# Spatial-reduction attention with a mixture of adapters: another order of the first batch's loads, scores and slots

## The chip, the cores and the metric

The kernel runs on one core of a Trainium2 chip. The metric is the device time of one execution in microseconds (us). Five engines run side by side, each through its own instructions in program order: TensorE (PE, with its weight loads listed as PEld), VectorE (DVE), ScalarE (ACT), GpSimd (POOL) and SyncE (SP, which here issues DMAs). They meet through semaphores. TensorE's products land in PSUM, and VectorE or ScalarE fetches them from there.

## The reference

Two layers, one behind the other. The first is attention whose keys and values are 4x4 means of a feature map times a matrix; keys and values are the same. The second is a mixture of eight low-rank adapters of which each token uses the two with the highest logits.

```python
B, C, Hh, Ww = (4, 128, 384, 32)          # q: (B, 12288, 128), kv: (B, 384, 32, 128)
kv_pool = kv.reshape(B, H // r, r, W // r, r, C).mean(axis=(2, 4))   # r = 4: 768 keys
kv_flat = kv_pool.reshape(B, -1, C) @ w_sr
s = (1 / sqrt(C)) * (q @ kv_flat^T);  a = softmax(s);  x = a @ kv_flat
...
logits = x @ w_gate                        # 8 adapters of rank 16
topk = the two largest;  w = softmax over these two
out = x + sum over the two of  w * (x @ A[e]) @ B[e]
```

## The kernel before, in words

**Tiling.** The 4 x 12288 queries are cut into 96 chunks of 512 (24 for each batch), and four chunks make a group of 2048 whose transposed queries lie in one qT tile. The 768 keys of a batch are three blocks of 256. A *score unit* `scores(k, r)` is chunk k against key block r: two matmuls of 128x512 into one of two score buffers `sg`, and one exponential of 128x1024 on ACT into `em[k]`. A chunk has three units. `attend(k, s)` multiplies a quarter of the chunk's `em` with the values `vx` (6 matmuls; 24 for the chunk) into the accumulator `acc`, of which there is only one. `normalize` (DVE: rinv, xn) frees it again. The columns behind the values give the softmax denominator and the logits' differences.

**A chunk's way after that.** `top` finds the largest logits (DVE, four MAX8). `route` and `gates` make the weights `gw`, for pairs of chunks on POOL with one tanh on ACT (chunks 0 and 1 on DVE). When a chunk *enters*, `transposes` turns its xn and the previous chunk's hg through PE into PSUM and one copy (DVE, line 346, or ACT, line 344) brings both back as `tts`. `down` (h_ps) multiplies with A and waits for this copy, `gate` (DVE, hg) multiplies with `gw`, a slot later `up` (d_ps) multiplies with B and `finish` adds and stores (DVE, osb, and a DMA on SP).

**Slots.** The main loop (line 430) runs one slot for each k. Its order on PE: first score unit; transposes; second unit; `up`; a quarter of the attend of the chunk before; third unit; `down`; three quarters of the attend. Everything is issued under `keep`, which holds an engine's instructions in the order of the program. Which chunks are attended and which enter in a slot is worked out ahead by the dictionaries `att` and `enter` (lines 413 to 426). Before the change the prologue does all three units of chunks 0 to 3, and the loop begins at slot 4. Slot 4 attends chunk 0, slot 5 chunk 1, slots 6, 7 and 8 two chunks each, and from slot 9 on slot k attends chunk k-1. Chunks enter six slots behind, and slots 73, 74 and 76 take two at a time.

**Prologue.** The loads go out on SP (lines 126 to 136): group 0 of q in one DMA of 1 MB, the 24 pieces (256 KB) of the first batch's kv, group 1 of q in four pieces. Groups 0 and 1 of q are transposed on PE in fp32 (`turn_q`, copies on ACT, line 117; group 1 partly inside slots 4 to 6); later groups are cast by a POOL DMA (`cast_q`) and transposed by an SP DMA (`load_qT`). For each key block DVE adds rows (line 184), PE transposes and sums the rest in PSUM (`keys`, kpT_ps), DVE scales (kpT), `keys2` makes kfT and `values` makes vx. The projection of w_sr and w_gate (lines 146 to 157) comes first of all on PE. Batches 1 to 3 are prepared by POOL and in later slots; the sums of batch 1 go to POOL from slot 8 on (line 506).

Of the kernel before, what the change touches and what calls it, by code (L numbers as in the profile page):

```python
# [10 lines left out]
FP32 = mybir.dt.float32  # L11
BF16 = mybir.dt.bfloat16
# [3 lines left out]
ALU = mybir.AluOpType  # L16
# [4 lines left out]
def kernel(  # L21
# [10 lines left out]
    nc = tc.nc  # L32
    P = 128
    B, N, C = q.tensor.shape
# [17 lines left out]
    kvpool = ctx.enter_context(tc.tile_pool(name="kvpool", bufs=3))  # L52
    per_b = ctx.enter_context(tc.tile_pool(name="per_b", bufs=2))
    qpool = ctx.enter_context(tc.tile_pool(name="qpool", bufs=4))
    ppool = ctx.enter_context(tc.tile_pool(name="ppool", bufs=7))
    xpool = ctx.enter_context(tc.tile_pool(name="xpool", bufs=1))
    rpool = ctx.enter_context(tc.tile_pool(name="rpool", bufs=4))
    gpool = ctx.enter_context(tc.tile_pool(name="gpool", bufs=6))
    run = ctx.enter_context(tc.tile_pool(name="run", bufs=3))
    opool = ctx.enter_context(tc.tile_pool(name="opool", bufs=6))  # L60
    qdram = ctx.enter_context(tc.tile_pool(name="qdram", bufs=1, space=bass.MemoryType.DRAM))
    ps_s = ctx.enter_context(tc.tile_pool(name="ps_s", bufs=2, space=bass.MemoryType.PSUM))
    ps_a = ctx.enter_context(tc.tile_pool(name="ps_a", bufs=1, space=bass.MemoryType.PSUM))
# [4 lines left out]
    def mm(*a, **k):  # L68
        return keep(nc.tensor.matmul(*a, **k))  # L69

    def mtile(shape, dtype=FP32, name="mb"):
        return ps_m.tile(shape, dtype, tag="mb", name=name)
# [10 lines left out]
    def load_qT(g):  # L83
        t = qpool.tile([P, GT], BF16, tag="qT", name="qT")
        keep(nc.sync.dma_start(t.rearrange("c (j p) -> c j p", p=P),
                               q_bf[g].rearrange("(p j) c -> p (j c)", p=P), transpose=True))
        qT[g] = t
# [11 lines left out]
            keep(nc.sync.dma_start(kvr[b, h][:, r, x], src[:, :, x * 4 * C:(x + 1) * 4 * C]))  # L99


    def load_q(g, lo, hi):
        if g not in q_f:
            q_f[g] = xpool.tile([P, GT // P, C], FP32, tag=f"qf{g}", name="qf")
        src = q[0, g * GT:(g + 1) * GT].rearrange("(p j) c -> p j c", p=P)
        keep(nc.sync.dma_start(q_f[g][:, lo:hi], src[:, lo:hi]))

    def turn_q(g, m, engine):
        if m == 0:
            qT[g] = qpool.tile([P, GT], BF16, tag="qT", name="qT")  # L110
        ps = mtile([P, S, P], name="qT_ps")
        for i in range(S):
            mm(ps[:, i], q_f[g][:, m * S + i], id_f, is_transpose=True,
               start=(i == 0), stop=(i == S - 1))
        o = qT[g][:, m * T:(m + 1) * T].rearrange("p (s t) -> p s t", s=S)
        if engine is nc.scalar:
            keep(nc.scalar.copy(o, ps))
        else:
            keep(nc.vector.tensor_copy(o, ps))

    q_f = {}
    w_sr_sb = const.tile([P, C], FP32)
    keep(nc.scalar.dma_start(w_sr_sb, w_sr))
    w_gate_sb = const.tile([P, E], FP32)
    keep(nc.scalar.dma_start(w_gate_sb, moe_w_gate))
    load_q(0, 0, GC * S)
    for h in range(3):
        for r in range(4):
            for x in range(2):
                load_kv(0, h, r, x)  # L130
    for m in range(GC):
        load_q(1, m * S, m * S + S)
    b_f = const.tile([P, C], FP32)
    keep(nc.sync.dma_start(b_f, moe_B.rearrange("e r c -> (e r) c")))
    a_f = const.tile([P, P], FP32)
# [7 lines left out]
    make_identity(nc, id_f)  # L143
    id_bf = const.tile([P, P], BF16)
    nc.vector.tensor_copy(id_bf, id_f)
    wext = const.tile([P, VC], FP32)
    nc.vector.tensor_copy(wext[:, 0:C], w_sr_sb)
    wT_ps = mtile([P, C], name="wT_ps")
    mm(wT_ps, w_sr_sb, id_f, is_transpose=True, start=True, stop=True)
    wT = const.tile([P, C], FP32)  # L150
    nc.vector.tensor_copy(wT, wT_ps)
    w2_ps = mtile([P, E], name="w2_ps")
    mm(w2_ps, wT, w_gate_sb, start=True, stop=True)
    w2 = const.tile([P, E], FP32)
    nc.vector.tensor_copy(w2, w2_ps)
    nc.vector.tensor_scalar(wext[:, C:VC], w2[:, 0:E - 1], w2[:, E - 1:E], None,
                            op0=ALU.subtract)


    ring = [xpool.tile([P, 2, S, C + E], FP32, tag=f"xr{i}", name="xn") for i in range(6)]  # L160
# [6 lines left out]
    def prepare(b, adder):  # L167
# [18 lines left out]
        for h in range(3):  # L186
            if adder is nc.vector:
                sums.append([lambda h=h, r=r, x=x: pair_step(h, r, x)
                             for r in (0, 2) for x in range(2)])
                continue  # L190
            sums.append([lambda h=h, step=step, lo=lo: pool_step(h, step, lo, lo + 512)
                         for step in range(5) for lo in range(0, 1024 if step < 3 else 512, 512)])

        st = {}

        def keys(h):
            if h == 0:
                st["kpT"] = prep.tile([P, J, P], FP32, tag="kpT", name="kpT")
                kfT[b] = per_b.tile([P, J, P], BF16, tag="kfT", name="kfT")
            kpT = st["kpT"]  # L200
            ps = mtile([P, 2, P], name="kpT_ps")
            if adder is nc.vector:
                parts = [(r, i, c) for r in (0, 2) for i in range(2) for c in range(4)]
            else:
                parts = [(0, i, 0) for i in range(2)]
            for n, (r, i, c) in enumerate(parts):
                mm(ps[:, i], kvr[b, h][:, r, i, c * C:(c + 1) * C], id_f, is_transpose=True,
                   start=(n == 0), stop=(n == len(parts) - 1))
            keep(nc.vector.tensor_scalar(kpT[:, 2 * h:2 * h + 2], ps, 1.0 / 16.0, None,
                                         op0=ALU.mult))  # L210

# [23 lines left out]
            keep(nc.vector.tensor_copy(kfT[b][:, 2 * h:2 * h + 2], ps))  # L235

        for h in range(3):
            for f in (keys, keys2, values) if adder is nc.vector else (keys, values, turn):
                rest.append(lambda h=h, f=f: f(h))
        return sums, rest  # L240

# [5 lines left out]
    def scores(k, r):  # L247
        b = k // NB
        if r == 0:
            em[k] = ppool.tile([P, J, T], FP16, tag="em", name="em")  # L250
        rhs = qT[k // GC][:, (k % GC) * T:(k % GC + 1) * T]
        ps = ps_s.tile([P, 2, T], FP32, tag="sg", name="sg")
        for i in range(2):
            mm(ps[:, i], kfT[b][:, 2 * r + i], rhs, start=True, stop=True)
        keep(nc.scalar.activation(em[k][:, 2 * r:2 * r + 2], ps, AF.Exp, bias=0.0, scale=scale))  # L255

    def attend(k, s):
        b = k // NB
        if s == 0:
            acc[k] = ps_a.tile([P, S, 256], FP32, tag="acc", name="acc")  # L260
        o = acc[k][:, s, 0:VE]
        for j in range(J):
            mm(o, em[k][:, j, s * P:(s + 1) * P], vx[b][:, j, 0:VE], start=(j == 0),
               stop=(j == J - 1))
# [112 lines left out]
        for d in (em, acc, xn, xT, hgT, hp, hg, dp):  # L377
            d.pop(k, None)

    LA = 4  # L380

    for m in range(GC):
        turn_q(0, m, nc.scalar)
    sums, rest = prepare(0, nc.vector)
    for h in range(3):
        for item in sums[h]:
            item()
        rest[3 * h]()
        if h > 0:
            scores(2, h - 1)  # L390
        rest[3 * h + 1]()
        if h > 0:
            scores(3, h - 1)
            rest[3 * h - 1]()
        scores(0, h)
        scores(1, h)
    rest[8]()
    scores(2, 2)
    scores(3, 2)
    rest = []  # L400

    late = const.tile([P, 1], FP32)
    keep(nc.gpsimd.tensor_copy(late, q_f[1][:, GC * S - 1, 0:1]))
    for g in range(2, 4):
        cast_q(g)
    a_bf = const.tile([P, P], BF16)
    keep(nc.vector.tensor_scalar(a_bf, a_f, 0.5, None, op0=ALU.mult))
    b_bf = const.tile([P, C], BF16)
    keep(nc.vector.tensor_copy(b_bf, b_f))
    turn_q(1, 0, nc.scalar)  # L410


    att = {LA: [0], LA + 1: [1], LA + 2: [2, 3], LA + 3: [4, 5], LA + 4: [6, 7]}
    for k in range(8, NCHUNK):
        att[k + 1] = [k]
    normed = {}
    for t, ks in att.items():
        for k in ks:
            normed[k] = t + 1 if k == ks[-1] else t
    ready = {k: normed[first[k] + size[k] - 1] + 1 for k in range(NCHUNK)}  # L420
    enter, t, left = {}, LA, list(range(NCHUNK - 3))
    while left:
        can = [k for k in left if ready[k] <= t]
        enter[t] = can[:2] if t in [NB * (B - 1) + 1 + i for i in (0,1,3)] else can[:1]
        left = [k for k in left if k not in enter[t]]
        t += 1

    sums, rest = [], []
    kh, ku, kd, kdone = [], [], [], []
    for k in range(LA, NCHUNK):  # L430
        b, i = divmod(k, NB)
        ka = att.get(k, [])
        kx = enter.get(k, [])
        if k % GC == 0:
            g = k // GC
            if 2 <= g + 1 < B * NG:
                load_qT(g + 1)
            if 4 <= g + 2 < B * NG and g + 2 not in q_bf:
                cast_q(g + 2)
# [12 lines left out]
                route(first[kn])  # L452

        kn = [n for n in att.get(k - 1, []) if normed[n] == k]
        if k == LA:
            for s in range(S):
                attend(0, s)
            ka = []
        scores(k, 0)
        while later:  # L460
            later.pop(0)()
        for x_ in kd:
# [3 lines left out]
        pairs = [(kx[j] if j < len(kx) else None, kh[j] if j < len(kh) else None)  # L466
                 for j in range(max(len(kx), len(kh)))]
        for x_, h_ in pairs[:1]:
            transposes(x_, h_, nc.vector)
        for x_ in kd:  # L470
            gate(x_)
        if k + 1 in range(GC + 1, 2 * GC):
            turn_q(1, (k + 1) % GC, nc.scalar)
        scores(k, 1)
        for u_ in ku:
            up(u_)
            finish(u_)
# [6 lines left out]
            attend(ka[0], 0)  # L484
        for n in kn:
            after_norm(n)
        scores(k, 2)
        for x_ in kx[:1]:
            down(x_)
            gate(x_)  # L490
# [15 lines left out]
                sums.pop(0)()  # L506

    K = NCHUNK - 1
    assert kh == [K - 3] and ku == [K - 4], (kh, ku)

    def bank(pool):
# [184 lines left out]
```

## Time and profile before

| | |
|---|---|
| median of 3 runs | 398.32 us (398.23 to 399.0) |
| the profiled execution | 400.91 us, its span 398.9 us |
| mean granted TensorE clock | 0.996 |
| score unit's exponential, ACT 128x1024 | 288 times, 1023 ns |
| transposes' copy, DVE 128x1024 (line 346) | 89 times, 692 ns |
| the same copy on ACT (line 344): 128x1024, 128x512 | 1012 ns, 585 ns |
| copy of q, ACT 128x512 (line 117) | 8 times, 608 ns |
| DVE add of two kv rows, 128x512 (line 184) | 12 times, 688 ns |
| the chain's end by engine | PE 84%, DVE 5%, ACT 3%, DMA 3% |

The span runs from the first to the last instruction; the time of the execution also has what lies around it. Times in the views are microseconds from the start of the span. A line of the timeline has the start, the length, the engine, the line of the kernel, the operation, what it writes and reads, how many instructions were merged, and in brackets how long the engine had been idle before and what ended that.

### The profile page before, as it was taken

The page shows a single profiled execution, that of the slowest core. Times are in us where ns is not written, and L with a number is a line of the kernel's source. Part 1 is how long each engine was busy: PE and PEld are TensorE (multiplying, and loading weights), DVE is VectorE, ACT ScalarE, POOL GpSimd, SP SyncE. Part 2 cuts the span into 40 slices and gives each one's busy share as a digit, 9 for nine tenths or more (in the row PEclk, how much of TensorE's full clock was granted, in tenths as well). Part 3 has the DMA queues.
Part 4 walks back from the last instruction along what each step waited for, and adds up shares of the span by engine and source line. Part 5 has one row for each costly group of instructions (what it writes and reads, how often), then busy time and mean ns, then how long its engine had stood idle before and what let it go on. Part 6 is the DMA issues. An engine that isn't in the chain of part 4 may idle for free.

```text
span 398.9 us, 11605 instructions
## 1 busy us (share of the span) xinstructions
PE 372.5 (93%) x4515; PEld 300.3 (75%) x4589; DVE 324.6 (81%) x945; ACT 297.0 (74%) x375; POOL 198.9 (50%) x457
## 2 busy tenths in 40 slices
PE   3898889999999999999999998999999899999993
PEld 2656777888878787887887886878786678788882
DVE  2553678899998889889898887988898788888885
ACT  2379467877787887787787876886878778888873
POOL 0010069887523486786523485787523344434443
PEclk9999999999999999999999999999999999999998
DMA  8988757993689999982679799993762847734113
GB/s 294 375 247 220 203 128 210 308 232 107 158 133 330 330 242 278 167 188 82 162 175 325 150 260 156 308 249 105 159 158 81 161 152 166 158 126 116 63 73 134
DMA packets 71463, 76.46 MB, mean 192 GB/s; under 512 B 49936, under 2 KB 50704, under 8 KB 70928
## 3 DMA queue, kind: packets, MB, share of 16 engines
q1 hardware_dynamic: 70272, 63.98, 57.6%
q0 software_dynamic: 704, 11.54, 15.0%
q8 instruction: 36, 0.59, 0.6%
q10 hardware_dynamic: 432, 0.20, 0.2%
q14 instruction: 19, 0.16, 0.1%
HBM read 50.53 MB, written 36.70 MB: 219 GB/s over the span
## 4 chain that ended last, share of the span: by engine, by line
PE 84%; DVE 5%; ACT 3%; DMA 3%; issue 2%; SPq 1%; POOL 0%; ACTq 0%; DVEq 0%; POOLq 0%
PE acc L69 33%; PE sg L69 24%; PE tt_ps L69 11%; PE h_ps L69 6%; PE d_ps L69 6%; ACT em L255 2%; DMA w_sr_sb<-in_w_sr_dram 1%; PE kpT_ps L69 1%; SPq L99 1%; DMA kvr<-in_kv_dram 1%; DVE rinv L268 1%; PE v_ps L69 1%; DVE xn L273 1%; DVE tts L346 1%; PE kfT_ps L69 1%
## 5 line engine op out<-in xcount | busy, mean ns | idle before, releaser
L255 ACT ACTIVATE em<-sg 128x1024 f16<-128x1024 f32 x288 | 280.4, 1023 | 78.7 <-PE sg L69 59.6
L69 PE MATMUL acc<-vx,em 128*128 128x136 f16 x2280 | 165.8, 223 | 2.8 <-issue 1.6
L69 PE MATMUL sg<-qT,kfT 128*128 128x512 bf16 x502 | 155.1, 379 | 2.9 <-ACT em L255 2.3
L69 PEld LDWEIGHTS <-em 128*128 128x128 f16 x2304 | 143.8, 98 | 4.9 <-DVE xn L273 2.2
L69 PEld LDWEIGHTS <-tts 128*128 128x128 bf16 x740 | 56.4, 98 | 46.1 <-issue 2.8
L273 DVE TENSOR_TENSOR xn<-acc,rinv 128x540 f32<-128x540 f32 x95 | 68.4, 720 | 3.3
L303 POOL TENSOR_TENSOR over<-xn,srt 128x64 f32<-128x64 f32 (+1 forms) x116 | 30.2, 281 | 79.7 <-DVE srt L291 79.7
L360 DVE TENSOR_TENSOR hg<-h_ps,gw 128x512 bf16<-128x512 f32 x93 | 64.3, 691 | 6.9 <-PE h_ps L69 0.2
L180 POOL TENSOR_TENSOR kvr<-kvr 128x512 f32<-128x512 f32 x54 | 67.3, 1271 | 0.0
L373 DVE TENSOR_TENSOR osb<-d_ps,xn 128x512 f32<-128x512 f32 x91 | 62.6, 691 | 0.6 <-PE d_ps L69 0.6
L346 DVE COPY tts<-tt_ps 128x1024 bf16<-128x1024 bf16 (+1 forms) x90 | 62.0, 689 | 1.2 <-ACT em L255 0.7
L324 POOL TENSOR_TENSOR gw<-th,over 128x64 f32<-128x64 f32 (+1 forms) x58 | 16.9, 291 | 73.1 <-ACT th L322 72.9
L69 PEld LDWEIGHTS <-kfT 128*128 128x128 bf16 x576 | 45.6, 98 | 6.3 <-issue 3.9
L268 DVE RECIPROCAL rinv<-acc 128x4 f32<-128x4 f32 x95 | 17.4, 183 | 35.8 <-PE acc L69 34.9
L69 PEld LDWEIGHTS <-xn 128*128 128x128 bf16 x384 | 29.1, 98 | 20.9 <-DVE xn L273 0.4
L69 PE MATMUL h_ps<-a_bf,tts 128*128 128x128 bf16 x372 | 36.0, 219 | 2.1 <-ACT tts L344 0.7
L69 PE MATMUL d_ps<-b_bf,tts 128*128 128x128 bf16 x364 | 35.2, 219 | 2.7 <-DVE tts L346 1.1
L69 PE MATMUL tt_ps<-id_bf,xn 128*128 128x128 bf16 x372 | 35.9, 219 | 1.2
L69 PE MATMUL tt_ps<-id_bf,hg 128*128 128x128 bf16 x368 | 35.6, 219 | 0.3 <-DVE hg L360 0.3
L291 DVE MAX8 srt<-xn 128x8 f32<-128x8 f32 x380 | 34.2, 153 | 0.2
L69 PEld LDWEIGHTS <-hg 128*128 128x128 bf16 x384 | 25.6, 98 | 1.3 <-DVE hg L360 0.5
L309 POOL TENSOR_SCALAR over<-over 128x64 f32<-128x64 f32 (+1 forms) x58 | 19.3, 333 | 5.2
(83 smaller groups left out, 198.1 us busy)
## 6 DMA issues: line engine op xcount, KB each, us to landing
out_dram<-osb SPq DMA_DIRECT2D x94, 256.0 KB, 3.6
kvr<-in_kv_dram SPq DMA_DIRECT2D x36, 512.0 KB, 6.8
qbf<-in_q_dram POOLq DMA_DIRECT2D x22, 512.0 KB, 7.5
kvr<-in_kv_dram SPq DMA_DIRECT2D x24, 256.0 KB, 5.3
qf<-in_q_dram SPq DMA_DIRECT2D x1, 1024.0 KB, 5.3
qf<-in_q_dram SPq DMA_DIRECT2D x4, 256.0 KB, 5.4
out_dram<-osb SPq DMA_DIRECT2D x3, 128.0 KB, 2.3
qT<-qbf SPq DMA_TRANSPOSE x22, 8.9
```

Source lines behind the costliest of these rows:

```text
L69: return keep(nc.tensor.matmul(*a, **k))
L180: keep(adder.tensor_tensor(u[:, lo:hi], u[:, lo:hi], v[:, lo:hi], op=ALU.add))
L255: keep(nc.scalar.activation(em[k][:, 2 * r:2 * r + 2], ps, AF.Exp, bias=0.0, scale=scale))
L268: keep(nc.vector.reciprocal(ri, acc[k][:, :, VC]))
L273: keep(nc.vector.tensor_tensor(x[:, :, 0:VC], acc[k][:, :, 0:VC], ri.unsqueeze(2).broadcast_to([P, S, VC]), op=ALU.mult))
L291: keep(nc.vector.max(srt[k0][:, m, s], xn[k][:, s, C:C + E]))
L303: keep(eng.tensor_tensor(d, lg, so[:, :, i].unsqueeze(2).broadcast_to([P, n, 8]), op=ALU.subtract))
L309: keep(eng.tensor_scalar(mask, mask, 0.0, None, op0=ALU.is_ge))
L324: keep(eng.tensor_tensor(w[:, 0:n], th, mask, op=ALU.mult))
L346: keep(nc.vector.tensor_copy(sb[:, lo:hi], ps[:, lo:hi]))
L360: keep(nc.vector.tensor_tensor(hg[k].rearrange("p s (e r) -> p (s e) r", e=E), hp[k].rearrange("p s (e r) -> p (s e) r", e=E), gw[k0][:, m ...
L373: keep(nc.vector.tensor_tensor(osb, dp[k], xn[k][:, :, 0:C], op=ALU.add))
```

## The change

The first batch is done in another order.

- **Loads:** the first key block goes ahead of everything (column half by column half); behind it come groups 0 and 1 of q in eight pieces of 256 KB, in tiles of the pool `opool`; then blocks two and three.
- **Spin:** fourteen matmuls of an identity with a tile of zeros stand first on PE. Their result isn't read.
- **Projection:** it becomes a function `project`, called among the first scores.
- **q:** `turn_q` transposes into halves of the one `acc` tile, and DVE makes all eight copies.
- **Key rows:** of a block's second column half only rows 0 and 1 are added on DVE; rows 2 and 3 are both transposed and summed on PE (20 transposes instead of 16, three sums instead of four).
- **Prologue's scores:** block one for chunks 0 to 7, block two for chunks 0 to 4, block three for chunk 0: 14 units instead of 12.
- **Slots:** the loop begins at slot 1 and each slot k attends chunk k-1. Slots 1 to 11 hold two score units, taken from a list; from slot 12 on three, as before. In slots below 12 the copy of the transposes is made by ACT.
- **Entering:** the planner's dictionaries follow: chunks enter four slots behind, and only slot 74 takes two.
- `load_qT(2)` is issued ahead of the loop, `late` (which holds back the first casts) waits for the last kv piece, and `ppool` and `opool` have 8 buffers.

```diff
-    ppool = ctx.enter_context(tc.tile_pool(name="ppool", bufs=7))
+    ppool = ctx.enter_context(tc.tile_pool(name="ppool", bufs=8))
...
-    opool = ctx.enter_context(tc.tile_pool(name="opool", bufs=6))
+    opool = ctx.enter_context(tc.tile_pool(name="opool", bufs=8))
...
+    def load_q(g, m):
+        q_f[g, m] = opool.tile([P, S, C], FP32, tag="osb", name="qf")
         src = q[0, g * GT:(g + 1) * GT].rearrange("(p j) c -> p j c", p=P)
-        keep(nc.sync.dma_start(q_f[g][:, lo:hi], src[:, lo:hi]))
+        keep(nc.sync.dma_start(q_f[g, m], src[:, m * S:(m + 1) * S]))
...
+    def turn_q(g, m):
         if m == 0:
             qT[g] = qpool.tile([P, GT], BF16, tag="qT", name="qT")
-        ps = mtile([P, S, P], name="qT_ps")
+        if m % 2 == 0:
+            turned[g] = ps_a.tile([P, 2, S, P], FP32, tag="acc", name="qT_ps")
+        ps = turned[g][:, m % 2]
...
+        keep(nc.vector.tensor_copy(
+            qT[g][:, m * T:(m + 1) * T].rearrange("p (s t) -> p s t", s=S), ps))
...
+    load_first(0)
+    for g in range(2):
+        for m in range(GC):
+            load_q(g, m)
+    load_first(1)
+    load_first(2)
...
+    zero = const.tile([P, T], BF16)
+    nc.vector.memset(zero, 0.0)
+    for _ in range(14):
+        mm(mtile([P, T], name="spin_ps"), id_bf, zero, start=True, stop=True)
+
     wext = const.tile([P, VC], FP32)
...
+    def project():
+        keep(nc.vector.tensor_copy(wext[:, 0:C], w_sr_sb))
+        wT_ps = mtile([P, C], name="wT_ps")
+        mm(wT_ps, w_sr_sb, id_f, is_transpose=True, start=True, stop=True)
...
             if adder is nc.vector:
                 sums.append([lambda h=h, r=r, x=x: pair_step(h, r, x)
-                             for r in (0, 2) for x in range(2)])
+                             for r, x in ((0, 0), (2, 0), (0, 1))])
...
+        def turn_rows(h, x):
+            if x == 0:
+                st["ps"] = mtile([P, 2, P], name="kpT_ps")
+            rows = (0, 2) if x == 0 else (0, 2, 3)
+            for r in rows:
+                for c in range(4):
+                    mm(st["ps"][:, x], kvr[b, h][:, r, x, c * C:(c + 1) * C], id_f,
+                       is_transpose=True, start=(x == 0 and r == 0 and c == 0),
+                       stop=(x == 1 and r == 3 and c == 3))
...
+            if adder is nc.vector:
+                rest.append([lambda h=h: turn_rows(h, 0), lambda h=h: turn_rows(h, 1),
+                             lambda h=h: keys(h), lambda h=h: keys2(h), lambda h=h: values(h)])
+                continue
...
+    first_sums(0, 0, 1, 2)
+    prep_of(0, 0, 1, 2)
+    turn_q(0, 0)
+    prep_of(0, 3)
+    turn_q(0, 1)
+    scores(0, 0)
+    turn_q(0, 2)
+    scores(1, 0)
+    turn_q(0, 3)
+    project()
+    scores(2, 0)
+    turn_q(1, 0)
+    prep_of(0, 4)
+    scores(3, 0)
+    turn_q(1, 1)
+    scores(4, 0)
+    turn_q(1, 2)
+    turn_q(1, 3)
+    first_sums(1, 0, 1)
+    scores(5, 0)
+    prep_of(1, 0)
+    first_sums(1, 2)
+    scores(6, 0)
+    scores(7, 0)
+    prep_of(1, 1, 2, 3)
+    scores(0, 1)
+    first_sums(2, 0, 1)
+    prep_of(1, 4)
+    scores(1, 1)
+    scores(2, 1)
+    prep_of(2, 0)
+    first_sums(2, 2)
+    scores(3, 1)
+    prep_of(2, 1, 2)
+    scores(4, 1)
+    prep_of(2, 3)
+    prep_of(2, 4)
+    scores(0, 2)
 
     late = const.tile([P, 1], FP32)
-    keep(nc.gpsimd.tensor_copy(late, q_f[1][:, GC * S - 1, 0:1]))
+    keep(nc.gpsimd.tensor_copy(late, kvr[0, 2][:, 3, 1, 0:1]))
...
+    load_qT(2)
+
+    units = [(5, 1), (1, 2), (2, 2), (6, 1), (3, 2), (7, 1), (4, 2), (5, 2), (6, 2), (7, 2)]
+    units += [(k, r) for k in range(8, NCHUNK) for r in range(R)]
+
+    def unit():
+        scores(*units.pop(0))
+
+    att = {k: [k - 1] for k in range(1, NCHUNK + 1)}
...
-        enter[t] = can[:2] if t in [NB * (B - 1) + 1 + i for i in (0,1,3)] else can[:1]
+        enter[t] = can[:2] if t == NB * (B - 1) + 2 else can[:1]
...
-    for k in range(LA, NCHUNK):
+    for k in range(1, NCHUNK):
...
-        scores(k, 0)
+        unit()
...
-            transposes(x_, h_, nc.vector)
+            transposes(x_, h_, nc.scalar if k < 12 else nc.vector)
...
-        scores(k, 1)
+        unit()
...
-        scores(k, 2)
+        if k >= 12:
+            unit()
```

## The prediction

> **What bounds the kernel now.** I read the page's busy shares and slices first, then the table of stretches, then the chain of waits in order of time, then the timeline of two places: the first 30 us, and the slots around 315 us.
>
> ```profile
> span 398.9 us, 11605 instructions
> PE 372.5 (93%) x4515; PEld 300.3 (75%) x4589; DVE 324.6 (81%) x945; ACT 297.0 (74%) x375; POOL 198.9 (50%) x457
> ...
> ACT  2379467877787887787787876886878778888873
> ...
> PE 84%; DVE 5%; ACT 3%; DMA 3%; issue 2%; SPq 1%; POOL 0%; ACTq 0%; DVEq 0%; POOLq 0%
> ```
>
> TensorE is the bound of nearly the whole span. The stretches (length, then busy time of PE, PEld, DVE, ACT, POOL, granted clock, DMA share, GB/s) show where it isn't:
>
> ```profile
> 0.00:5.00 5.00, 0.00 (x0) 0.00 (x0) 0.06 (x1) 1.49 (x2) 0.91 (x12) 1.00 0.63 209
> 35.00:40.00 5.00, 4.79 (x45) 3.54 (x46) 1.45 (x5) 5.00 (x8) 0.00 (x0) 1.00 1.04 297
> 45.00:50.00 5.00, 4.35 (x58) 3.51 (x60) 3.69 (x15) 1.92 (x2) 0.55 (x2) 1.00 0.36 106
> 60.00:70.00 10.00, 9.89 (x125) 7.87 (x125) 8.85 (x26) 7.32 (x11) 9.35 (x18) 1.00 0.76 210
> ```
>
> From slot 9 on PE is 99% busy. So only three places can pay: the prologue (to 29.95, where slot 4 begins), slots 4 to 8, and slots 73 to 79, as the chain shows (start, length, what):
>
> ```profile
> 62.68 1.06 PE acc L69 x18
> 66.35 1.06 PE acc L69 x18
> 69.96 1.06 PE acc L69 x18
> ...
> 296.43 1.07 PE acc L69 x18
> 300.04 0.71 PE acc L69 x12
> ...
> 331.20 1.06 PE acc L69 x18
> ```
>
> This piece comes 2.71 us after its slot's first score matmul (59.98 in slot 10), so slot 12 starts at 67.25. A plain slot is 3.61. From slot 72's piece (296.43) to slot 80's (331.20) eight slots take 34.77 instead of 28.88: three slots with two chunks entering cost 5.9 together.
>
> **The change, step by step.** After slot 11 both kernels have done 36 score units and attended chunks 0 to 10, and from slot 12 the slots hold the same work. So the forecast is: slot 12's new start against 67.25, less what slots 73 to 79 give back.
>
> *Loads.* The same 8.4 MB, in another order. Old: the eighth kv piece, with 1.05 MB of q ahead, lands at 12.3 (the sum at 12.35 waited for it), the fifteenth at 17.2: 0.71 us a piece. With no q ahead the first block is in 1.05 MB, or four pieces, earlier: 9.4. Query pieces then land from 10.1 to 15.1, blocks two and three are complete at 20.8 and 26.4 as before. Three more SP issues of about 0.6 hide behind the landings that pace that queue (uncovered: 1.8). The `late` copy now waits for the last kv piece, about 26.1 either way. SP waits for the first cast at load_qT(2); behind it stand only batch 1's loads and the first stores, slots away. Deeper ppool and opool issue nothing.
>
> *Fourteen spin matmuls.* PE has nothing to do before about 6.4. Half a score unit is 0.21, so 3.0 at full rate, 6.0 at half; from 2.2 they end at 5.2 to 8.2. Cost 0 to 0.6, taken 0. The weight loads of the first transposes took 229 ns until 12.9 and 140 ns after, though the granted clock reads 1.00 throughout.
> The Trainium skill (TensorE: Matmul & The Clock Gate, Part 4: PE-mode transpose) says that transposes don't count as activity and don't bring the full clock; here it rose after 5.7 us of nearly nothing but transposes, so the row disagrees. By the page, the 28 transposes between spin and first scores would fall back to slow ones, up to 28 x 0.09 = 2.5 us; by the row, none.
>
> *First scores.* Rows now need a sum of rows 0 and 1 only in the second half, and 12 transposes of 0.14 there: PE finishes them at about 10.4, kpT starts at 10.6. From there the old trace gives the rest:
>
> ```profile
> 12.35 0.69 DVE L184 TENSOR_TENSOR kvr<-kvr 128x512 f32<-128x512 f32 x1 [0.84 <-DMA kvr<-in_kv_dram]
> ...
> 14.08 0.42 DVE L209 TENSOR_SCALAR kpT<-kpT_ps 128x256 f32<-128x256 f32 x1 [1.04 <-PE kpT_ps L69]
> ...
> 15.36 0.42 DVE L216 CAST kfT<-kfT_ps 128x256 bf16<-128x256 f32 x1 [0.85 <-PE kfT_ps L69]
> ...
> 16.49 1.94 ACT L255 ACTIVATE em<-sg 128x1024 f16<-128x1024 f32 x2 [4.53 <-PE sg L69]
> ```
>
> kpT to first exponential is 2.41, so 13.0 instead of 16.49: 3.5 won.
>
> *The way to block two's scores.* From here I place the instructions one after another on their engines, in program order, with the rows' durations. Eight 128x512 copies of q leave ACT (0.61 each) for DVE. DVE has no such row; its 128x256 casts take 0.425 and the 128x512 adds out of PSUM 0.69, so 0.69. From 11.8 to block two's first sum DVE must do seven of these (4.83), the kfT and vx copies (0.87) and the projection (0.23 + 0.29 + 0.17 + 0.23): 6.6. It also waits. All turns go through the single acc buffer, two to a tile, so the third, fifth and seventh wait for both copies before them and then need 0.57 + 0.15 on PE: 2.0 of DVE waiting. The projection, formerly at 6.3 beside the first loads, puts a PE-DVE-PE-DVE trip among the scores: 0.7. Smaller gaps behind v_ps and score units: 0.9. So 22.1; without any waits 18.5, the lower bound. Then two sums (1.24), 4 transposes (0.56), units (6,0) and (7,0) (0.86), 12 transposes (1.68), 0.15: kpT at 26.6, exponential (0,1) at 29.0. The data lay there at 20.8; the old kernel had block two's scores at 21.39.
>
> *Block three.* From that unit's matmul (28.3): v_ps and (1,1) to 29.8, unit (2,1) waits for a score buffer until 30.1, then 8 transposes, (3,1), 12 transposes: 33.7. kpT, kfT and its copy: (0,2) at 35.5, slot 1 at 36.0. The same placing of the old prologue gives slot 4 at 30.98 against 29.95 in the trace, so I take 1.0 off: **slot 1 at 35.0** (31.4 if no wait on DVE were real).
>
> *Slots 1 to 11.* Dropping a unit leaves PE 3.61 - 0.43 = 3.18. But the copy behind the transposes goes to ACT, in line behind the slot's first exponential, and `down` needs it before three quarters of the attend. A row of that kind exists:
>
> ```profile
> 314.89 1.01 ACT L344 COPY tts<-tt_ps 128x1024 bf16<-128x1024 bf16 x1 [0.36 <-PE tt_ps L69]
> ...
> 315.96 0.40 PE L69 MATMUL h_ps<-a_bf,tts 128*128 128x128 bf16 x4 [0.53 <-ACT tts L344]
> ```
>
> So: first score to exponential 0.67, exponential 0.95 (back to back), copy 1.01, hand-over 0.05, `down` 0.22, 18 attends 1.07: 3.97, 0.8 above PE's work. Slots 4, 7, 9, 11: 3.97 each. Slots 8 and 10 have a tanh (0.15) between: 4.12. Slot 3 copies a half (0.585): 3.55. Slot 6 is 3.55 plus 0.4, because the tanh of pair 2 waits on ACT for POOL after slot 5. Slot 5, no `down`: 2.73. Slot 1 waits 0.88 for a score buffer: 3.17. Slot 2 has two units and an attend that waits 0.3 for its accumulator: 2.58. Sum 40.1 (old, slots 4 to 11: 37.3). **Slot 12 at 75.1, 7.8 late.** Bounds: with the copy hidden 33.2 (slots 4 and 7 to 11 at 3.18, slot 6 at 2.95, slot 3 at 2.73); with no overlap of back-to-back exponentials (0.07 on each of 22) 41.6.
>
> *Later.* Chunks enter two slots earlier, so two of three doubled entries go. One costs what rows of slots 73, 74, 78 and 79 show over 3.61: 0.22 + about 1.0 + 0.22 + 0.51 = 1.9. Given back: 5.9 - 1.9 = 4.0. Entering two slots earlier also takes a cover off: in even slots POOL's gw is ready 2.72 into the slot, where DVE starts hg at 2.81. Old slack two slots, new slack 0.09. I cost it at nothing; DVE's own reserve is 0.28 a slot (3.61 less 0.18 + 0.72 + 4 x 0.09 + 3 x 0.69).
>
> **Sum:** +7.8 - 4.0 = +3.8 on the span of 398.9, whose execution took 400.91. That lies 2.6 above the median of 398.32; the difference carries over: **402.1**.
>
> **Rivals.**
> *The first batch keeps pace with its loads* (faster). If DVE's waits shrink to what the loads demand, block three is done 26.4 + 0.7 + 2.4 = 29.5 and slot 1 starts near 30: -5, 397.1. For: ACT gives up eight copies; 3.5 us are won at the front. Against: everything is in program order on two engines that take turns. It decides if block two's sums start by 18.
> *The ACT copy is hidden* (faster). If it ends 1.9 into the slot, slots 1 to 11 take the 33.2 of above: -6.9, 395.2. For: ACT is only 74% busy. Against: the 0.53 wait at 315.96.
> *hg waits for gw* (slower still). If the gates come 0.4 late in even slots, 0.12 beyond the reserve over 30 slots is +3.6, and behind POOL's four 1.24 us sums up to 2 in a few: 406 to 408. It decides from 0.3 late. For: slack 0.09; against: in the last batch chunks already enter without slack and slots stay 3.61.
> *The spin does not bring the clock*: transposes stay 0.09 slower until 12.9, +0.6 to +1.5, 403.
>
> **How the numbers follow.** Forecast 402.1, own range 399.8 to 404.5, chance 0.57; first rival 0.13, second 0.08, third 0.14, spin 0.08. One 1.6 us gap marked "issue" at 246.15, if it goes, is inside the own range. Half measures of the first two rivals end between 398 and 400. I leave a tenth on each side: 397 to 406.5. A measurement tells 0.2%, 0.8 us, from no change: below 397.5 0.19, within 0.05, above 0.76.
>
> **What would show it.** First exponential near 13 and slot 1 near 35, block two's first sum near 21 to 22 although its rows lie there by 18; h_ps released by ACT tts about 0.9 late in slots 4 and 6 to 11; slot 12 near 75; one bulge near slot 75. Wrong if slot 1 starts before 32, if these slots take 3.3, or if hg lists POOL gw as a releaser.

## The result, and the profile after

| | before | after |
|---|---|---|
| median | 398.35 us (398.23 to 399.0, 4 runs) | 411.14 us (410.69 to 411.75, 4 runs) |
| ratio to before, 95% interval | | 1.0319 (1.0301 to 1.0337) |
| profiled execution, its span | 400.91 us, 398.9 us | 411.75 us, 409.9 us |
| mean granted TensorE clock | 0.996 | 0.997 |

The changed kernel is 12.8 us slower. The forecast was 3.8 slower, with 406.5 as the upper end of the range: the side was right, the size was not. The experiments ran on three chips (e1 to e4, e5 to e8, e9 to e11), where some executions of every kernel were disturbed and took several us more; beside each ratio the text therefore names the lowest group of times, which for the kernel before was 398.4 to 399.5 on all three.

The page's first part and the row of ACT in the slices, after:

```profile
span 409.9 us, 11667 instructions
PE 376.7 (92%) x4541; PEld 300.5 (73%) x4615; DVE 325.3 (79%) x945; ACT 298.2 (73%) x373; POOL 199.6 (49%) x457
...
ACT  1055776777777788778777887786877888888874
...
PE 81%; DMA 6%; DVE 5%; ACT 4%; issue 2%; SPq 1%; POOL 0%; ACTq 0%; DVEq 0%; POOLq 0%
PE acc L69 30%; PE sg L69 22%; PE tt_ps L69 10%; PE h_ps L69 6%; PE d_ps L69 5%; DMA qT<-qbf 4%; PE kpT_ps L69 2%; ACT em L281 2%; PE spin_ps L69 1%; ACT tts L370 1%; PE v_ps L69 1%; DMA kvr<-in_kv_dram 1%; DVE rinv L294 1%; PE qT_ps L69 1%; PE kfT_ps L69 1%
```

Busy times hardly moved: DVE has 0.7 us more, ACT 1.2, PE 4.2 (the spin is 5.7, so the rest has less). The other 6.8 us of the span's 11.0 are idle time of PE (33.2 instead of 26.4). The loss lies at the start: ACT stands at 5 tenths or less in the first four slices of 10.2 us, where before it stood at 2, 3, 7 and 9. The chain's shares would mislead here: PE's part fell from 84% to 81% and DMA's rose from 3% to 6%, but 4 of these 6 (qT<-qbf) are one transposed load far behind the prologue, for which PE waits 2.05 us at 278 (last section). The timeline of the first 20 us shows it one instruction at a time (start, length, engine, line, what; in brackets the idle time before and what ended it):

```profile
4.84 0.69 DVE L197 TENSOR_TENSOR kvr<-kvr 128x512 f32<-128x512 f32 x1 [3.68 <-DMA kvr<-in_kv_dram]
...
7.28 0.69 DVE L197 TENSOR_TENSOR kvr<-kvr 128x512 f32<-128x512 f32 x1 [1.75 <-DMA kvr<-in_kv_dram]
8.68 0.69 DVE L197 TENSOR_TENSOR kvr<-kvr 128x512 f32<-128x512 f32 x1 [0.71 <-DMA kvr<-in_kv_dram]
9.29 0.22 DVE L151 CAST id_bf<-id_f 128x128 bf16<-128x128 f32 x1
...
9.57 5.66 PE L69 MATMUL spin_ps<-zero,id_bf 128*128 128x512 bf16 x14 [9.57 <-DVE id_bf L151]
...
15.16 2.38 PE L69 MATMUL kpT_ps<-id_f,kvr 128*128 128x128 f32 x20
...
19.91 1.02 ACT L281 ACTIVATE em<-sg 128x1024 f16<-128x1024 f32 x1 [16.80 <-PE sg L69]
```

The reader is to see the order on DVE. The identity that the spin multiplies with is cast (line 151) *behind* the three sums of block one, and the sums wait for loads. So the spin, which stands first on PE, starts at 9.57 instead of about 2, and keeps the finished rows of block one waiting until 15.2. The first exponential comes at 19.91; the old kernel had it at 16.49.

From there the delay is carried. In the chain of waits slot 12's attend piece begins at 85.00, 2.70 after the slot's first score matmul, which puts slot 12 at 82.30 (67.25 before, 75.1 forecast):

```profile
69.51 1.06 PE acc L69 x18
73.43 1.06 PE acc L69 x18
77.48 1.07 PE acc L69 x18
81.39 1.08 PE acc L69 x18
...
85.00 1.07 PE acc L69 x18
...
311.83 1.06 PE acc L69 x18
...
342.45 1.07 PE acc L69 x18
```

The first five pieces are those of slots 8 to 12: 3.92, 4.05 and 3.91 apart where the forecast had 4.0 to 4.1 and PE's own work is 3.18; the fourth gap, 3.61, is that of a plain slot. Slot 80's piece (342.45) stands 11.25 behind the old one (331.20), slot 12's stood 15.04 behind: 3.8 came back in between. From slot 72's piece (311.83) to slot 80's the kernel takes 30.62, before 34.77, so the slots there give back 4.15; 0.4 of it is lost again on the way, where after has the wait of 2.05 at 278 and before a stall of 1.6 at 246.

### The profile page after: what moved, and what is told of

The parts are those of the page before. It is cut to its first block, busy times and chain, and to the rows that moved or that the text cites. A ratio compares the mean times of both kernels' runs of the same rounds, so it can differ in the third digit from the quotient of the medians.

```text
span 409.9 us, 11667 instructions
## 1 busy us (share of the span) xinstructions
PE 376.7 (92%) x4541; PEld 300.5 (73%) x4615; DVE 325.3 (79%) x945; ACT 298.2 (73%) x373; POOL 199.6 (49%) x457
## 4 chain that ended last, share of the span: by engine, by line
PE 81%; DMA 6%; DVE 5%; ACT 4%; issue 2%; SPq 1%; POOL 0%; ACTq 0%; DVEq 0%; POOLq 0%
PE acc L69 30%; PE sg L69 22%; PE tt_ps L69 10%; PE h_ps L69 6%; PE d_ps L69 5%; DMA qT<-qbf 4%; PE kpT_ps L69 2%; ACT em L281 2%; PE spin_ps L69 1%; ACT tts L370 1%; PE v_ps L69 1%; DMA kvr<-in_kv_dram 1%; DVE rinv L294 1%; PE qT_ps L69 1%; PE kfT_ps L69 1%
## 5 line engine op out<-in xcount | busy, mean ns | idle before, releaser
L372 DVE COPY tts<-tt_ps 128x1024 bf16<-128x1024 bf16 x84 | 58.1, 692 | 2.4 <-PE tt_ps L69 2.4
```

Source lines behind the costliest of these rows:

```text
L372: keep(nc.vector.tensor_copy(sb[:, lo:hi], ps[:, lo:hi]))
```

## Experiments

The first theory (A in the expectations) says that the spin's place, not its length, cost the unforeseen time: `keep` pins an instruction behind those before it on its engine, the identity's cast isn't kept and nothing pins the sums behind it, so it slid behind instructions that wait for loads. Its rival is that the spin itself is the loss, wherever it stands. A second group of runs asks for the price of two forecast costs (ACT's copy, the turns of q), a third for what the lag, the spin and the loads' order are worth.

### e1: identity and zeros kept in place

```diff
-    nc.vector.tensor_copy(id_bf, id_f)
+    keep(nc.vector.tensor_copy(id_bf, id_f))
-    nc.vector.memset(zero, 0.0)
+    keep(nc.vector.memset(zero, 0.0))
```

> The one difference to the changed kernel: the cast of the identity and the zeros are held in place on DVE, ahead of the first key sums, so the spin can start near 2 us and not at 9.57. Theory A (the late spin holds up the whole prologue): first score matmul near 12.5 instead of 19.27, everything behind it as much earlier, 404.3 us (404 to 405). Theory B (the prologue is bound by loads or by the DVE/PE chain anyway, the spin is hidden): first score earlier, but slot 1 within 2 us of before, 409 us or more.

Measured: 404.88 us median (lowest group 404.6 to 405.0, a fourth execution 412.75), ratio to before 1.0141 (1.0100 to 1.0182). Its timeline:

```profile
1.51 0.23 DVE L151 CAST id_bf<-id_f 128x128 bf16<-128x128 f32 x1 [0.65 <-POOL id_f masks.py:199]
...
2.06 6.02 PE L69 MATMUL spin_ps<-zero,id_bf 128*128 128x512 bf16 x14 [2.06 <-DVE zero L153]
...
9.46 0.69 DVE L197 TENSOR_TENSOR kvr<-kvr 128x512 f32<-128x512 f32 x1 [0.76 <-DMA kvr<-in_kv_dram]
...
14.43 1.02 ACT L281 ACTIVATE em<-sg 128x1024 f16<-128x1024 f32 x1 [11.31 <-PE sg L69]
```

Two kept instructions bring 6.3 us between the medians. The first exponential moves by 5.48 (19.91 to 14.43), slot 12 by 5.46 (to 76.84); the rest lies behind slot 12, where after's profile has its wait of 2.05 and e1's has none. The zeros were early in after as well (0.89), so it is the cast that counts. Theory A holds, and its rival falls: the spin ends at 8.08, inside the 5.2 to 8.2 that the prediction gave it, and hides behind the loads, since the last awaited sum starts only at 9.46. The first score came 1.3 later than theory A had expected (13.80, not 12.5).

### e2: the spin taken out

```diff
-    for _ in range(14):
-        mm(mtile([P, T], name="spin_ps"), id_bf, zero, start=True, stop=True)
```

> The changed kernel without its fourteen spin matmuls. Theory A1 (the spin, in time, saves slow transposes): the first 20 transposes run at 0.23 us, first score near 14.5, 406 us, slower than with an early spin by 1.5 to 2. Theory A2 (the spin buys nothing even when early): the same as with the early spin, 404 to 404.5. Theory B (spin hidden): no change, 411.

Measured: four executions of 405.47, 405.64, 411.48 and 569.47 us, ratio 1.0207 (1.0097 to 1.0318). The two low ones are 5.6 under after's median, and 0.8 over e1's lowest group. So the late spin was the loss. That an early one is better than none isn't shown here, as 0.8 is less than the interval can tell; e7 asks again.

### e3 and e4: the copy of the transposes on DVE

```diff
-            transposes(x_, h_, nc.scalar if k < 12 else nc.vector)
+            transposes(x_, h_, nc.vector)
```

e3 has this on top of e1, e4 on the changed kernel alone.

> Early identity as in the run before it, and the copies of the transposes in slots below 12 on DVE instead of ACT. My slot sum says slots 4 and 6 to 11 fall from 3.9-4.1 to 3.0-3.9, DVE-bound near 3.3 in the last four: slots 1 to 11 in 35.1 instead of 40.0, so 4.9 below the run with the early identity, 399.4 us. Rival: DVE, now at 3.3 of work a slot, and the single accumulator take it back: less than 2 us gained.

> The changed kernel with only the copies of slots below 12 moved from ACT to DVE, the spin as late as it was. If the two costs add, 4.9 below the changed kernel: 406.2 us. If the late prologue had hidden part of the slots' cost, less.

Measured: e3 400.35 us median (lowest group 399.0 to 399.4), ratio 0.9999 (0.9963 to 1.0036); e4 405.70 (lowest 404.95), ratio 1.0185 (1.0107 to 1.0262). Slot 12 starts 5.76 earlier than in e1 and 5.38 earlier than in the changed kernel, and the lowest times are some 5.5 lower, so this cost and the spin's add up. Slots 6 to 11 shrink from 3.91 to 4.06 each to 2.95 to 3.18, which is PE's own 3.18. In the changed kernel the wait reads so:

```profile
64.00 1.01 ACT L370 COPY tts<-tt_ps 128x1024 bf16<-128x1024 bf16 x1
...
65.06 0.40 PE L69 MATMUL h_ps<-a_bf,tts 128*128 128x128 bf16 x4 [0.79 <-ACT tts L370]
```

A part is given back behind slot 12: slot 13 takes 4.13 in e3 (74.69 to 78.82) where a plain slot takes 3.61. With the shorter slots two chunks' gates come while POOL still has sums of batch 1 in its queue, and there the third rival appears:

```profile
71.15 1.26 POOL L191 TENSOR_TENSOR kvr<-kvr 128x512 f32<-128x512 f32 x1
72.38 0.56 POOL L329 TENSOR_TENSOR over<-xn,srt 128x64 f32<-128x64 f32 x2
...
74.69 0.59 PE L69 MATMUL sg<-qT,kfT 128*128 128x512 bf16 x2
74.75 0.32 POOL L351 TENSOR_TENSOR gw<-gw,over 128x64 f32<-128x64 f32 x1
...
75.11 0.69 DVE L386 TENSOR_TENSOR hg<-h_ps,gw 128x512 bf16<-128x512 f32 x1 [1.32 <-POOL gw L351]
...
75.85 0.34 PE L69 MATMUL tt_ps<-id_bf,hg 128*128 128x128 bf16 x3 [0.34 <-DVE hg L386]
```

The gates of the pair start at 72.38, behind a sum of 1.26, and DVE's hg waits 1.32 for them; PE, which turns this hg in slot 13, has to wait in its turn, and slot 14 starts 0.5 late.

### e5 and e6: separate PSUM buffers for the turns of q

e5 is e3 with the odd turns in a buffer of their own; e6 is e5 with their copies on ACT.

```diff
-        ps = turned[g][:, m % 2]
+        ps = mtile([P, S, P], name="qT_ps") if m % 2 else turned[g][:, 0]
...
-        keep(nc.vector.tensor_copy(
-            qT[g][:, m * T:(m + 1) * T].rearrange("p (s t) -> p s t", s=S), ps))
+        o = qT[g][:, m * T:(m + 1) * T].rearrange("p (s t) -> p s t", s=S)
+        keep(nc.scalar.copy(o, ps) if m % 2 else nc.vector.tensor_copy(o, ps))
```

(The change of the copy, the two removed and the last two added lines, is in e6 alone.)

> Early identity and DVE copies in the slots (the 399 us version), and now every second turn of q has a PSUM buffer of its own instead of the other half of the acc tile. In that version each turn waited for the DVE copy of the turn before it, also within one tile, 1.44 us a turn. Theory (the shared tile serialises PE and DVE): turns 0.7 to 1.1 us apart, block two's first sum some 2 to 3 us before 24.15, 397 us. Rival (DVE's own 6.6 us of work sets it): less than 0.8 gained.

> As the run with the separate buffers, and every second copy of q is made by ACT. By the durations, block two's first exponential comes about 1.2 us earlier again and slot 1 with it: 395.5 to 396.5 us, faster than the kernel before. Rival: ACT's copies delay the first exponentials as much as DVE gains: no change to the run with separate buffers.

Measured: e5 396.58 us median (lowest group 396.2 to 396.6), ratio 0.9936 (0.9892 to 0.9980). e6 397.47 median of executions that scatter more, its lowest group 394.7 to 395.3, ratio 0.9918 (0.9875 to 0.9962). Block two's first sum is where they differ; the timelines of e3, e5 and e6, one line of each:

```profile
24.15 1.88 DVE L197 TENSOR_TENSOR kvr<-kvr 128x512 f32<-128x512 f32 x3
```

```profile
21.17 1.88 DVE L197 TENSOR_TENSOR kvr<-kvr 128x512 f32<-128x512 f32 x3
```

```profile
19.84 1.89 DVE L197 TENSOR_TENSOR kvr<-kvr 128x512 f32<-128x512 f32 x3
```

In e1 and e3 nearly every turn waits for the copy of the turn before, although the two write different halves of one tile. In e1's timeline PE and DVE take turns at 1.44 us a turn (0.66 and 0.69 with two hand-overs):

```profile
14.75 0.66 PE L69 MATMUL qT_ps<-id_f,qf 128*128 128x128 f32 x4 [0.35 <-DVE qT L120]
...
15.44 0.69 DVE L120 CAST qT<-qT_ps 128x512 bf16<-128x512 f32 x1 [0.75 <-PE qT_ps L69]
```

With buffers of their own the sum comes 2.98 earlier, and slot 12 starts at 68.10 instead of 71.08. With half of the copies on ACT it starts at 66.76: 0.5 before the old kernel's, and with what slots 73 to 79 give back this version is faster than before, by 3.3 us after its ratio's middle (1.5 to 5.0 after its interval) and by some 4 between the lowest groups. That e6 is faster than e5 is seen at slot 12 (1.34) and in the three lowest times (394.7 to 395.3 against 396.2), but the medians don't tell the two apart.

### e7: e6 without the spin

The same edit as e2, on top of e6.

> As the run with copies on both engines, without the fourteen spin matmuls. If the spin, started in time, brings the clock: the first 20 transposes at 0.23 instead of 0.14, first score 0.8 to 1.8 us later and the whole run as much slower, 396.5 to 397.5. If not: the same within 0.3.

Measured: 397.94 us median (lowest group 396.0 to 396.8), ratio 0.9945 (0.9897 to 0.9993). The last transposes ahead of the first score, in e6 and then in e7 (weight loads, then matmuls):

```profile
10.05 1.29 PEld L69 LDWEIGHTS kpT_ps<-id_f,kvr 128*128 128x128 f32 x12 [0.92 <-DVE kvr L197]
10.06 1.53 PE L69 MATMUL kpT_ps<-id_f,kvr 128*128 128x128 f32 x12 [0.68 <-DVE kvr L197]
```

```profile
10.26 2.42 PEld L69 LDWEIGHTS kpT_ps<-id_f,kvr 128*128 128x128 f32 x12 [0.71 <-DVE kvr L195]
10.26 2.82 PE L69 MATMUL kpT_ps<-id_f,kvr 128*128 128x128 f32 x12 [0.30 <-DVE kvr L195]
```

Without the spin twelve transposes take 1.29 longer; the first exponential comes at 15.46 instead of 13.96 and slot 12 at 68.27 instead of 66.76. Of these 1.5 us 0.2 are a later load (the twelve start at 10.26, not 10.06), so an early spin is worth 1.3 at slot 12. The lowest times differ by 1.3 too, though the intervals of the two ratios overlap. The granted clock reads 1.00 in both.

### e8: the old lag of six slots

```diff
-    enter, t, left = {}, 1, list(range(NCHUNK - 3))
+    enter, t, left = {}, 6, list(range(NCHUNK - 3))
...
-        enter[t] = can[:2] if t == NB * (B - 1) + 2 else can[:1]
+        enter[t] = can[:2] if t in [NB * (B - 1) + 1 + i for i in (0,1,3)] else can[:1]
```

This is on top of e3.

> Early identity and DVE copies (the 399 us version), but chunks enter six slots behind as in the kernel before, with two entering in slots 73, 74 and 76. Leaves out nothing; only the planner differs. By my sum of the later slots: slot 12 starts about 2 us earlier (two chunks' transposes, down and up fewer, and no hg waiting for gw in slots 12 and 14), slots 73 to 79 take 31.2 instead of 27.5, together 1 to 2.7 us slower, 400 to 402. Rival (the short lag costs more in gates that come late than it gives back): 398.5 or less.

Measured: 402.81 us median (lowest group 401.2 to 401.3), ratio 1.0082 (1.0036 to 1.0128): 2.0 over e3. Slots 74 to 77 take 4.63, 4.68, 4.56 and 5.51 again instead of 3.84, 4.40, 3.83 and 4.12 (in after), 3.2 in all, and slots 73 to 79 together 31.2 instead of 27.0, 4.1 in all; against it slot 13 is back at 3.61 (no wait of hg), and slots 3 to 6 are together 1.4 shorter (12.34 in e3, 10.95 in e8), since no chunk enters in slots 3 to 5. That leaves 2.2, beside 2.0 measured. So the shorter lag does pay, but part of what it saves at the end it costs at the start.

### e9 and e10: why the first loads are late; e11: the changed kernel again

In e6 block one's last awaited sum starts 1.3 later than the forecast's loads allow (9.31, not about 8.0; in the changed kernel's own profile 8.68). e9 loads a block's pieces row by row as the old kernel did, e10 loads block one in four pieces of 512 KB. Both are on top of e6.

```diff
-        for x in range(2):
-            for r in range(4):
+        for r in range(4):
+            for x in range(2):
                 load_kv(0, h, r, x)
```

```diff
+        if h == 0:
+            for r in range(4):
+                load_kv(0, 0, r, None)
+            return
```

> e6 with one part changed: a key block's pieces are loaded row by row (both column halves of a row, then the next row), as in the kernel before, instead of half by half. In e6 the DMA engines move 256, 244, 252 GB/s in the microseconds 4 to 7, where the kernel before moves 434, 329, 377; block one's last awaited sum starts at 9.31, the first exponential at 13.96. Theory L1 (the half-by-half order is what the memory serves slowly): over 330 GB/s from 4 to 7, the last awaited sum at 8.6 or earlier although it now waits for the seventh piece instead of the sixth, first exponential 12.7 to 13.4, time 0.5 to 1.3 under e6. Rival L2 (the first microseconds are slow for another reason, the order has no part): rates as in e6, the sum waits one piece longer (about 10), first exponential 14.3 to 14.8, time 0.3 to 0.9 over e6.

> e6 with block one alone loaded in four pieces of 512 KB, each a row with both halves. L1: as for the row order, rates over 330 GB/s from 4 to 7, first exponential 12.7 to 13.4, time 0.5 to 1.3 under e6. L2: rates as in e6, first sum later (it needs two pieces of 512 KB, about 6.2 instead of 4.82), first exponential 14 to 14.8, time 0 to 0.9 over e6. If four issues instead of eight bring the q pieces forward, the second turn of q no longer waits for its piece; that is worth under 0.3.

> The changed kernel itself, beside the other runs and on their chip, so that the differences of e1, e2 and e4 from it are between runs of one place. Both theories of the first experiments expect its undisturbed executions at 410.7 to 411.8; 409 or less would make the identity's gain (6.3) smaller by as much.

Measured: e9 399.36 us median (most of its lower times at 397.3 to 397.9, one at 395.55), ratio 0.9970 (0.9946 to 0.9994); e10 397.71 (lower times 396.5 to 398.2), ratio 0.9977 (0.9952 to 1.0003); by the ratios both some 2 us over e6, with intervals that still touch e6's (e10's profile is of an execution of 403.49). e11: 410.53 lowest (then 412.80, 414.69 and 416.75), ratio 1.0341 (1.0302 to 1.0379), so the changed kernel costs the same on this chip. The stretches (length, clock, DMA share, GB/s) of e6, e9 and e10:

```profile
4.00:5.00 1.00, 1.00 0.92 256
5.00:6.00 1.00, 1.00 0.95 244
6.00:7.00 1.00, 1.00 0.93 252
```

```profile
4.00:5.00 1.00, 1.00 1.01 238
5.00:6.00 1.00, 1.00 0.89 264
6.00:7.00 1.00, 1.00 0.89 291
```

```profile
4.00:5.00 1.00, 1.00 1.04 401
5.00:6.00 1.00, 1.00 0.95 356
6.00:7.00 1.00, 1.00 0.95 365
...
8.00:9.00 1.00, 1.00 1.06 240
9.00:10.00 1.00, 1.00 0.77 193
```

L1 falls: the order of the halves changes little in the rates. L2's forecast for e10 falls too: in pieces of 512 KB the same block does move at 356 to 401 GB/s, but the gain is gone by 8 to 10 us, where the q pieces of 256 KB follow at 193 to 240, and its first sum needs two whole rows (6.38 instead of 4.82). In e6 pieces of 256 KB run at 375 GB/s from 3 to 4 us, at about 250 from 4 to 7, and at 379 to 414 from 12 us on; why is open.

e9 also lost more than its later sum: its first exponential is at 16.36, 2.4 behind e6. In e10, whose last two sums start at the same time (9.77; 9.76 in e9), it is at 15.03, so 1.1 of the 2.4 go with the later sums and 1.3 with a slow PE. The sixteen transposes behind 1.9 us of idle PE took 3.17, against 2.13 in e10:

```profile
10.51 3.17 PE L69 MATMUL kpT_ps<-id_f,kvr 128*128 128x128 f32 x16 [1.90 <-DVE kvr L197]
```

```profile
10.52 2.13 PE L69 MATMUL kpT_ps<-id_f,kvr 128*128 128x128 f32 x16 [2.56 <-DVE kvr L201]
```

PE was slow again there after a whole spin, and in e10 it wasn't, after a longer idle time. One profile of each doesn't settle what decides.

## Why the prediction was right in its side and wrong in its size

**The step that failed** is "Fourteen spin matmuls ... from 2.2 they end at 5.2 to 8.2. Cost 0 to 0.6, taken 0". Its length (up to 6.0) was right, and so was the cost of a spin that starts there: in e1 it takes 6.02 and ends at 8.08, later than the 6.4 given for the cover, but the last awaited sum starts only at 9.46, so it costs nothing. What failed is the start at 2.2: that the two operands of the spin, made by DVE, are there at once because they stand first in the program. Both stand outside `keep`, unlike the sums behind them, and in the changed kernel the identity's cast ran at 9.29 behind sums waiting for DMA. That cost 5.5 at slot 12 and 6.3 in the run time (e1 against after). With the spin early, e1's 404.6 to 405.0 stand within 3 us of the forecast and still 6 above the kernel before, so the side was no luck.

**Loads**, too early by 1.4. With the spin early, the first exponential is at 14.43, not 13.0: the last awaited sum, the sixth piece's, starts at 9.46 instead of about 8.0 (the 9.4 of the eighth piece less two of 0.71). In after's own profile it starts at 8.68, in the other runs with this order at 9.1 to 9.6. The step "0.71 us a piece" came from pieces further back in the queue; block one's moved at 238 to 297 GB/s from 4 to 7 us in after, where 0.71 us a piece is 369. Of the 3.5 us that the first scores were to win, 2.06 were there in e1 and none in after.

**The way to block two's scores**, mechanism right, some waits too few. The prediction let the third, fifth and seventh turn wait for the accumulator; in e1 nearly every turn waits, since the two halves of the tile are one buffer to the program's semaphores. From the first exponential to block two's first sum it had 9.1 (13.0 to 22.1); after has 9.74, e1 9.77. The 1.0 taken off slot 1 for a placing that had been too slow on the old prologue was not there: from first exponential to slot 1 it forecast 22.0, and after took 22.8 (19.91 to 42.7).

**Slots 1 to 11**: predicted 40.1, measured 39.6. The slots with ACT's copy were put at 3.97 and 4.12 and took 3.91 and 4.05; the wait named (h_ps for ACT's tts) is in the trace with 0.2 to 0.8 on PE, and e3 and e4 take it away and with it 5.4 to 5.8. The second rival (the copy is hidden) is refuted.

**Given back at the end**: predicted 4.0, measured 4.15 between the pieces of slots 72 and 80, with bulges in slot 75 (4.40) and slot 77 (4.12). From slot 12 on it is 3.8, for the stalls named above. In e8 the lag is worth 2.0 net in the run time.

**The carry-over** to the median, mis-sized by some 1.9. The profiled execution of before lay 2.56 above the median, after's only 0.61 above. Other executions of the kernel before have spans near 397.0 in the experiments, not 398.9; that the 1.6 us gap marked "issue" is most of the difference is likely but not shown, as only this one execution has a trace. What belonged to one execution was carried over as if it belonged to both kernels. Together: the profiled execution took 411.75, not the 404.7 that the sum implies, 7.0 more (5.5 spin, 1.4 loads; the smaller terms, the stalls among them, leave 0.1), and with 1.9 here that makes the 9.0 between 402.1 and 411.1. The split between spin and loads is good to somewhat under 1 us, since the loads of after's profile came 0.8 before e1's and e4 against e3 puts the late spin at 5.84.

**The other rivals.** "The first batch keeps pace with its loads" did not happen, and its condition (block two's sums by 18) was not reached even in e6 (19.84); but its mechanism is real, and e5 and e6 buy 4.3 us at slot 12 with it. "hg waits for gw" does not bind in after: in a plain even slot gw is ready 2.67 into the slot and hg starts at 2.81, and DVE's hg waits for it once, 0.4 us, as it did before. It binds once the slots become shorter (e3 to e7, slot 12's hg, so that PE waits in slot 13), behind POOL's sums as priced: in e3 four times, 2.4 us on DVE in all, and not in thirty slots. "The spin does not bring the clock" was wrong, but its price of 0.6 to 1.5 is what a missing clock costs (e7: 1.3).

**Transposes and the clock.** The prediction set the Trainium skill (TensorE: Matmul & The Clock Gate, Part 4: PE-mode transpose) against a row: the page says that transposes do not bring the full clock. e7 sides with the row: with no spin, the weight loads of the transposes take 0.20 each at 10.26 and 0.165 at 12.66, behind 2.4 us of nothing but fp32 transposes, and 0.14 from 13.9 on (the first line stands in full under e7):

```profile
12.66 0.66 PEld L69 LDWEIGHTS qT_ps<-id_f,qf 128*128 128x128 f32 x4
...
13.92 0.57 PEld L69 LDWEIGHTS qT_ps<-id_f,qf 128*128 128x128 f32 x4
```

**What remains of the change.** In the run times the shorter lag wins about 2 and an early spin perhaps 0.8 to 1.3, and the new order brings the first exponential 2 us forward. The late spin loses 6.3, ACT's copy some 5.5, the shared tile 2.8 and the copies that ACT gave up to DVE 1.3 at slot 12. With these four mended (e6) the lowest group of times is 394.7 to 395.3 us, against 398.4 to 399.5 before.

## What to carry to other kernels

Before a start-up trick is costed at nothing, follow its operands back to their engines: a two-instruction preparation that is free to slide in an in-order queue can end up behind whatever waits there, and the engine that needs its result waits with it (PE until 9.57 here). Give PE and its fetching engine two separate PSUM buffers, not two halves of one tile, where they are to overlap. Before the difference between two kernels is carried from one profile to a median, compare the profile's span with other executions of the same kernel.

## What the runs showed of the hardware that had not been expected

- The matmuls of the spin took 0.43 us each at first and 0.21 later, at a granted clock of 1.00 throughout. The faster rate came within the spin in some executions (14 in 4.70, e8, where the starts are 0.21 apart from 5.30 on; 5.07, e10) and only at its end in others (6.02, e1; 6.11, e9), so from 3 to 6 us after its start.
- DMAs of 256 KB that were the first on their queue moved 238 to 297 GB/s from 4 to 7 us (after, e6, e9), and up to 400 later; 512 KB pieces in the same place moved 356 to 401 in the one profile that has them (e10).
- Single stalls of 1.4 to 5.3 us come and go between executions, two kinds of them: 1.6 marked "issue" in before's slot 59 (first line, the page of before; 2.9 in e7, 1.7 in e8, 3.3 in e10), and in after's slot 64 a wait for a transposed load (second line). In e11, the same kernel, that wait is 5.3 at another place (266.8); e6 and e10 have one of 1.4 and 2.1. Why is open:

```profile
L69 PE MATMUL acc<-vx,em 128*128 128x136 f16 x2280 | 165.8, 223 | 2.8 <-issue 1.6
...
278.42 0.39 PE L69 MATMUL sg<-qT,kfT 128*128 128x512 bf16 x1 [2.05 <-DMA qT<-qbf]
```
